# A block of their own for the turning products, ten tiles of P, and P V capped at three groups a block

## The chip, the cores and the metric

The kernel runs on one core of a Trainium2 chip. What counts is the device time of one execution in microseconds (us), as a median over runs. A core has five engines with queues of their own: TensorE (PE, with its weight loads shown apart as PEld), VectorE (DVE), ScalarE (ACT), GpSimd (POOL) and SyncE (SP), which here only issues transfers. Matrix products are written to PSUM, which has eight banks of 128 partitions by 512 float32; all other operands lie in SBUF.

## The reference

A transformer block with modulation by a condition vector: 2048 rows of 512 values, attention with 32 heads of 16, then a token mixer and an MLP. The parts around the change are those of the attention:

```python
h = _layernorm(x, axis=-1) * (1 + ca) + sa
qkv = (h @ wqkv).reshape(B, S, 3, H, Dh).transpose(2, 0, 3, 1, 4)
q, k, v = qkv[0], qkv[1], qkv[2]
p = _softmax(jnp.einsum("bhqd,bhkd->bhqk", q, k) * (Dh ** -0.5), axis=-1)
o = jnp.einsum("bhqk,bhkd->bhqd", p, v)
x = x + ga * (o.transpose(0, 2, 1, 3).reshape(B, S, D) @ wo)
```

After it, `x` goes through the second modulated layernorm and the mixer with its MLP (four more weight matrices), which the kernel calls the tail.

## The kernel before, in words

**Stages.** A prologue makes Q, K and V with their low parts and stores them to DRAM (`Qs`, `Ks`, `Vs`). Then comes the attention loop, which fills most of the time, and the tail in four chunks of 512 rows, of which the first one starts 30 steps before the attention ends.

**Units, steps, blocks.** The attention has 64 units: 4 chunks of 512 queries by 16 pairs of heads. A unit has 16 steps, one for each 128 keys (`NKT`), so there are 1024 steps, and a step has two halves, one for each head of the pair. The loop goes in blocks of three half steps (`GRP`). In a block PE does two things, one after the other:

- *rows* (`row_pair`): for each half step the scores S of this step (L1026, tile `sc`) and, 24 steps ahead, a product whose row maxima a later unit needs (L999, tile `mb`). Both use half of PE's rows and run side by side. Each writes a bank of its own out of seven that are shared (`sm`, `Slots`, tags s0 to s6).
- *columns* (`pv_part`): groups of P V, which lag behind by two blocks. A group is four products of 32 columns each, side by side. There is a group of the high part for every step (L1100) and one of the low part for every two steps (L1097). All of a unit add up in the eighth bank (tile `pv`, tag v).

The other engines empty the banks. DVE takes the maximum of each `mb` (L995). ACT takes the exponential of each `sc` into a tile of P (L1022). POOL makes the low part of P in place (L1075), or ACT does it (`p_low`) where the plan has POOL later. Tiles of P are a ring of six, and in the steps of `WIDE` (264 to 983) two more lie in tail buffers that are not yet in use (`xbs`), eight in all. The list `pvs` says in which order groups of P V come and from which half step on each may run; in `WIDE` a low part is put off by `LOWLAG` = 3 half steps more.

**The end of a unit.** After the last group of P V, ACT copies the sums from bank v to the tile `ac` (`ac_copy`, L1117), and the next unit's P V may write the bank. Four float32 products with the constant `smat` turn the sums into rows of queries (`o_fin`, L1127, tile `ot`). They stand in a generator that the plan lets go where PE has room and one of the seven shared banks is free, so they land behind the P V of some block, 1 to 12 us after `ac`. ACT then copies the result to `sm` (L1134), DVE takes the reciprocal `rc` (L1142), and POOL writes the output of the unit (L1138).

**Order.** All engines' instructions are put in order at build time by a planner (`Sched`) that carries a modelled time for each engine (`sch.T`), with planned costs. `crit` puts an instruction in its engine's queue at once; chains (`sch.chain`) and generators (`sch.add`) fill what is left. On the chip each engine keeps its order and waits on semaphores.

**Loads.** `before(s)` (L1600) puts in the loads on SP's queue: Q and K two units ahead at the first step of a unit (`load_unit`), V (`load_v`) six steps ahead of its unit. When a unit's maxima are known (`max_fin`), eight small transfers write the shift rows (`qtl<-nm`). K of a unit is first used 24 steps before the unit's scores. At step 884 a generator `tail_loads` (L1288) starts to load the tail's first things: three 1 MB pieces of weights (`wr`) on SP's queue, each `T0W` = 3000 ns of planned time after the other, and then four tiles `x1` of 256 KB on ACT's queue.

Of the kernel before, what the change touches and what calls it, by code (L numbers as in the profile page):

```python
# [8 lines left out]
F32 = mybir.dt.float32  # L9
# [3 lines left out]
I32 = mybir.dt.int32  # L13
# [28 lines left out]
PX = 270.0  # L42
XX = 170.0
XP = {"A": 280.0, "D": 200.0, "G": 200.0}
# [4 lines left out]
CROW, CCOL, CIN, CMID, COUT = 232.0, 240.0, 105.0, 95.0, 67.0  # L49
# [32 lines left out]
X1F = 6  # L82
# [1 line left out]
XBF = 4  # L84
XBT = 4
T0S = 30
T0L = 140
T0W = 3000.0
RATE3 = 1000.0
BURST3 = 1300.0  # L90
BF, BR = 2, 3
# [7 lines left out]
NPT = 6  # L99
# [7 lines left out]
LNC = 2  # L107
VP = 2
WIDE = range(S // CH * 64 + 8, 984)
LOWLAG = 3  # L110
XB = 4


# [219 lines left out]
def kernel(ctx, tc, A_x, A_wqkv, A_wo, B_w1, B_w2, B_w3, B_w4, c, w_mod, out):  # L333
    nc = tc.nc
    te, act, dve, pool, dma = nc.tensor, nc.scalar, nc.vector, nc.gpsimd, nc.sync
    x_d, out_d = A_x[0], out[0]
# [20 lines left out]
    def mark(key):  # L357
        return None, 0, lambda: done.add(key)
# [612 lines left out]
    def load_v(u):  # L971
        vst[u] = at.tile([P, NKT, 192], BF16, name="vst", tag="vst", bufs=2)
        sch.dma(dma.dma_start, vst[u], Vs[units[u][1]])

    sm = Slots(NSM)
    ptx = []
    e_exp, e_hi, e_low, v_free, acs = {}, {}, {}, [0.0], []

    def bank(nm):
# [23 lines left out]
    def new_pt(s):  # L1003
        if s in WIDE:
            i = pn[0] % (NPT + len(ptx)) - NPT
            pn[0] += 1
            if i >= 0:
                pt[s] = ptx[i]
                return
        pt[s] = at.tile([P, 2, CH], I32, name="pt", tag="pt", bufs=NPT)  # L1010

    def score_part(s, j):
# [97 lines left out]
    def ac_copy():  # L1110
        u, e = acs.pop()
        while u and ("ot", u - 1) not in done:
            sch.step()
        ac = at.tile([P, CH], F32, name="ac", tag="ac", bufs=1)
        vst.pop(u)
        acc = pv.pop(u)
        e = sch.crit("A", cA(), e + PX, lambda: act.activation(ac, acc, AF.Copy))  # L1117
        v_free[0] = e + XP["A"]
        sch.add(o_fin(u, ac, e + XP["A"]), 0)

    def o_fin(u, ac, ready):
        ci, pr = units[u]
        yield lambda: sch.T["P"] >= ready and sch.room()
        n = 2 * (DH + 1)
        b = dbank("ot")[:, :TPC * n]
        for t in range(TPC):
            te.matmul(b[:, t * n:(t + 1) * n], ac[:, t * P:(t + 1) * P], smat.rearrange("p j d -> p (j d)"), start=True, stop=True)  # L1127
            yield 110
        done.add(("ot", u))
        sm = at.tile([P, 8, DH + 1], F32, name="sm", tag="sm", bufs=2)  # L1130
        rc = at.tile([P, 8, 1], F32, name="rc", tag="rc", bufs=2)

        def sums():
            act.activation(sm.rearrange("p th d -> p (th d)"), b, AF.Copy)  # L1134
# [7 lines left out]
        sch.chain(("A", 170, sums), ("D", 90, lambda: dve.reciprocal(rc, sm[:, :, DH:DH + 1])), ("G", 350, fin),  # L1142
                  *([mark(("att", ci))] if pr == NP - 1 else []), prio=0, bank=b)


    GW = 130 + CH + 2
# [138 lines left out]
            for _ in mm3(b, wh[:, k, c], wl[:, k, c], A[:, k, 0, :n], A[:, k, 1, :n], k == 0, k == KT - 1):  # L1285
                yield nsq(n)

    def tail_loads():  # L1288
        rings["0"] = Ring(FRONT, [], "r")
        for _ in range(BR):  # L1290
            rings["0"].add([("wr", BR)])
            yield sch.wait(T0W)
        for t in range(TPC):
            x1t[t] = fa.tile([P, D], F32, name="x1", tag="x1", bufs=X1F)
            act.dma_start(x1t[t], x_d[t * P:(t + 1) * P])

    def tail(ci):
        end = ci == NC - 1
# [301 lines left out]
    def before(s):  # L1600

        nu, r = divmod(s + 32, 16)
        if r == 0 and 0 < nu < NU:
            ci, pr = units[nu]
            drain(("kq", pr // 4))
            if ci:
                drain(("q", pr // 8))
            load_unit(nu)
        nu, r = divmod(s + 6, 16)
        if r == 0 and 0 <= nu < NU:  # L1610
            drain(("v", units[nu][1] // 8))
            load_v(nu)
        if s == -12:
            unit_tiles(at, 2, dve, pool)

# [2 lines left out]
    blocks = [list(range(i, min(i + GRP, 2 * NS))) for i in range(-2 * LEAD, 2 * NS, GRP)]  # L1618
    pvs = []
    for s in range(0, NS, 2):  # L1620
        low = 2 * s + 2 + (min(LOWLAG, 2 * (NKT - 2 - s % NKT)) if s in WIDE else 0)
        pvs += [(2 * s, s, 0), (2 * s + 2, s + 1, 0), (low, s, 1)]
    pvs.sort(key=lambda x: x[0])
    due = 0.0
    for k, blk in enumerate(blocks + [[]] * (LAG + CPER)):
        if blk and blk[0] <= LENDS <= blk[-1]:
            sch.most = MOST
        for x in blk:
            if x % 2 == 0:
                if x == blk[0]:  # L1630
                    before(x // 2)
                if x >= 0 and x % 32 == 0:
                    drain(("shift", x // 32))
        if acs:
            ac_copy()
        row = [divmod(x, 2) for x in blk if x < 2 * NS]
        s0 = row[0][0] if row else 0
        col = []
        if k >= LAG and (k % CPER == 0 or not blk):

            x = (blocks[min(k - LAG, len(blocks) - 1)] or [-1])[-1]
            while pvs and pvs[0][0] < x and not (col and pvs[0][1] % NKT == 0 and not pvs[0][2]):
                col.append(pvs.pop(0)[1:])
        t, start = CIN, 0.0
        need = sum((s >= 0) + (s + LEAD < NS) for s, _ in row)
        sch.flush(need)
        banks = sorted(sm.t)
        n = 0
        for s, i in row:
            n += (s >= 0) + (s + LEAD < NS)  # L1650

            start = max(start, banks[n - 1 + 2 * (s < 0)] - t)
            t += CROW
        t += CMID
        for s, i in col:
            start = max(start, pv_ready(s, i) - t)
            t += CCOL
# [12 lines left out]
        sch.T["P"] += CMID  # L1670
        for s, i in col:
            pv_part(s, i)
        sch.T["P"] += COUT
        for e in "ADG":
            sch.misc(e, max(sch.T["P"], sch.T[e]) + TOLE[e])
        if s0 < 0:
            sch.fill(LEADB / 2 * len(blk))
        elif sch.gens:
            late = s0 >= NS - T0S
            due += RATE3 if late else RATE if s0 < NS // NC else RATE2  # L1680
            if due >= (BURST3 if late else BURST if s0 < NS // NC else BURST2):
                sch.fill(due)
                due = 0.0
        if 2 * (NS // NC) - 1 in blk:
# [12 lines left out]
            xnum = {"xn": 0, "xf": 0}  # L1697
            ptx += [xbs[:, 2 * i:2 * i + 2].bitcast(I32) for i in range(2)]
            big["A"] = big["A4"]
        if blk and blk[0] <= 2 * (NS - T0L) <= blk[-1]:  # L1700
            sch.add(tail_loads())
        if blk and blk[0] <= 2 * (NS - T0S) <= blk[-1]:
            sch.add(tail(0))
    if acs:
# [53 lines left out]
```

## Time and profile before

| What | us |
|---|---|
| median of 3 runs (2003.48 to 2003.94) | 2003.88 |
| the profiled execution | 2006.74 |
| its span, from the first instruction to the last | 2004.8 |
| DVE's maxima (L995), 2048 of 678 ns each, together | 1249.7 |
| ACT's exponentials (L1022), into the ring and into `xbs` | 890.3 + 200.0 |
| POOL's low parts (L1075), into the ring and into `xbs` | 1017.7 + 219.6 |
| busy in all: PE, DVE, ACT, POOL | 1939.3, 1656.6, 1519.9, 1551.9 |

Differences are made within the profiled execution; it took 2.9 us more than the median, 0.14%. Durations of instructions in a row overlap on an engine, so the distance from start to start tells what one costs in a run of them. In rows of the timeline, "x12" means that twelve instructions of one kind are drawn together, from the start of the first to the end of the last; the bracket at the end is the idle time before them with what ended it.

### The profile page before, as it was taken

How to read it: one execution, taken by the hardware profiler on the slowest of the kernel's cores; microseconds unless marked ns; L12 is line 12 of the kernel's file. 1: busy time of each engine (PE TensorE's matmuls, PEld its weight loads, DVE VectorE, ACT ScalarE, POOL GpSimd, SP SyncE). 2: the span in 40 equal slices, each digit the busy share in tenths (PEclk: the TensorE clock that was granted, in tenths of full speed). 3: DMA queues.
4: the chain of work that ended last, by engine and by line, in shares of the span. 5: the costliest groups of instructions: out<-in, count | busy, mean ns of one | idle time of the engine just before them, and what ended most of it. 6: DMA issues, size and time to landing. Idle time of an engine off the chain costs nothing.

```text
span 2004.8 us, 41627 instructions
## 1 busy us (share of the span) xinstructions
PE 1939.3 (97%) x14456; PEld 1161.6 (58%) x14456; DVE 1656.6 (83%) x2979; ACT 1519.9 (76%) x3100; POOL 1551.9 (77%) x1473
## 2 busy tenths in 40 slices
PE   7999999999999999999999999999998899999999
PEld 5755554554444444444444444444456788888998
DVE  6398888879999999999999999998976786656443
ACT  6438987768999999999999999998985545344443
POOL 6339998888999999999999999998995564435222
PEclk9989999999999999999999999999999999999999
DMA  8777665454444444444434343545415666553541
GB/s 292 235 196 190 158 177 175 131 135 124 94 83 97 87 94 90 91 91 90 94 87 95 86 96 85 107 115 128 94 38 213 225 235 266 217 205 112 199 152 69
DMA packets 185507, 277.99 MB, mean 139 GB/s; under 512 B 117105, under 2 KB 127857, under 8 KB 169009
## 3 DMA queue, kind: packets, MB, share of 16 engines
q1 hardware_dynamic: 181792, 267.20, 49.3%
q10 hardware_dynamic: 2304, 4.20, 0.6%
q0 software_dynamic: 1200, 3.93, 0.5%
q8 instruction: 115, 1.88, 0.4%
q14 instruction: 96, 0.78, 0.1%
HBM read 211.81 MB, written 62.91 MB: 137 GB/s over the span
## 4 chain that ended last, share of the span: by engine, by line
PE 61%; DVE 11%; DMA 4%; ACT 4%; POOL 3%; issue 2%; SPq 1%; ACTq 0%; POOLq 0%; DVEq 0%
PE mb L999 15%; PE sc L1026 10%; PE pv L1100 10%; DVE mx L995 8%; PE w L365 5%; PE w L361 5%; PE w L363 5%; PE pv L1097 4%; PE ot L1127 3%; ACT pt L1022 2%; DMA wr<-Ws 2%; POOL pt L1075 1%; PE xT L1261 1%; POOL trs L1370 1%; PE q L365 1%
## 5 line engine op out<-in xcount | busy, mean ns | idle before, releaser
L995 DVE TENSOR_REDUCE mx<-mb 128x1 f32<-128x512 f32 x2048 | 1249.7, 678 | 61.7 <-PE mb L999 54.0
L1075 POOL TENSOR_SCALAR pt<-pt 128x1024 f16<-128x1024 uint16 x773 | 1017.7, 1367 | 73.0 <-ACT pt L1022 72.6
L1022 ACT ACTIVATE pt<-sc 128x512 int32<-128x512 f32 x1688 | 890.3, 623 | 94.7 <-PE mb L999 65.6
L999 PE MATMUL mb<-kst,qtl 62*128 62x512 f32 x2048 | 787.0, 464 | 20.1 <-ACT pt L1022 7.7
L1026 PE MATMUL sc<-qtl,kst 64*128 64x512 f32 x2048 | 745.1, 451 | 3.7 <-DVE mx L995 1.8
L999 PEld LDWEIGHTS mb<-kst,qtl 62*128 62x128 f32 x2048 | 361.9, 193 | 263.3 <-ACT pt L1022 136.6
L1026 PEld LDWEIGHTS sc<-qtl,kst 64*128 64x128 f32 x2048 | 338.2, 185 | 189.2 <-DVE mx L995 116.9
L1100 PE MATMUL pv<-pt,vst 128*32 128x512 f16 x3376 | 318.6, 396 | 4.6 <-ACT ac L1117 4.6
L1479 POOL TENSOR_TENSOR g<-sq,g 128x256 fp32r<-128x256 f32 (+1 forms) x124 | 96.7, 784 | 189.7 <-ACT g L1478 176.0
L1075 POOL TENSOR_SCALAR xbs<-xbs 128x1024 f16<-128x1024 uint16 x165 | 219.6, 1363 | 4.4 <-ACT xbs L1022 4.3
L1022 ACT ACTIVATE xbs<-sc 128x512 int32<-128x512 f32 x360 | 200.0, 639 | 10.9 <-PE mb L999 9.5
L1100 PEld LDWEIGHTS <-vst 128*32 128x32 bf16 x4096 | 91.4, 94 | 182.9 <-issue 164.5
L1097 PE MATMUL pv<-pt,vst 128*32 128x512 f16 (+1 forms) x1688 | 173.0, 392 | 1.3 <-POOL pt L1075 1.3
L363 PE MATMUL w<-A,wr 128*128 128x256 f32 (+1 forms) x520 | 154.2, 297 | 0.3 <-DVE A L351 0.3
L361 PE MATMUL w<-A,wr 128*128 128x256 f32 (+1 forms) x520 | 154.2, 297 | 0.0
L365 PE MATMUL w<-A,wr 128*128 128x256 f32 (+1 forms) x520 | 154.0, 296 | 0.0
L1475 ACT ACTIVATE sq<-w 128x256 f32<-128x256 f32 (+1 forms) x130 | 52.0, 401 | 127.8 <-PE w L365 117.4
L361 PE MATMUL w<-wr,g 128*128 128x512 f32 x270 | 108.6, 402 | 3.0 <-DMA wr<-Ws 3.0
L365 PE MATMUL w<-wr,g 128*128 128x512 f32 x270 | 108.0, 400 | 3.1 <-POOL g L1479 3.1
L363 PE MATMUL w<-wr,g 128*128 128x512 f32 x270 | 107.7, 399 | 0.0
L1457 DVE SCALAR_TENSOR_TENSOR sq<-sq,w 128x256 f32<-128x256 f32 (+1 forms) x130 | 58.1, 449 | 55.6 <-ACT sq L1477 55.5
L363 PEld LDWEIGHTS w<-A,wr 128*128 128x128 f32 x520 | 99.6, 191 | 1.7 <-DVE A L351 0.5
(172 smaller groups left out, 2461.0 us busy)
## 6 DMA issues: line engine op xcount, KB each, us to landing
wr<-Ws SPq DMA_DIRECT2D x66, 1024.0 KB, 5.6
vst<-Vs SPq DMA_DIRECT2D x64, 768.0 KB, 5.2
kst<-Ks SPq DMA_DIRECT2D x126, 384.0 KB, 6.2
Ws<-wr SPq DMA_DIRECT2D x14, 1024.0 KB, 5.1
qtl<-Qs SPq DMA_DIRECT2D x128, 96.0 KB, 4.3
Vs<-vt SPq DMA_DIRECT2D x32, 384.0 KB, 4.3
Ks<-qk SPq DMA_DIRECT2D x16, 512.0 KB, 4.1
Qs<-qk SPq DMA_DIRECT2D x16, 512.0 KB, 3.0
```

What stands on the lines that cost most here:

```text
L361: te.matmul(o, lh, rh, start=first, stop=False)
L363: te.matmul(o, lh, rl, start=False, stop=False)
L365: te.matmul(o, ll, rh, start=False, stop=last)
L995: end = sch.crit("D", 605, e + PX, lambda: dve.reduce_max(mxs[u][:, j, g, c:c + 1], b, axis=AX.X))
L999: return ready, lambda: te.matmul(b, lhs, kst[u % 3][r, c * CH:(c + 1) * CH], start=True, stop=True), after
L1022: ea = sch.crit("A", 480, e + PX, lambda: act.activation(pt[s][:, j], b, AF.Exp))
L1026: return ready, lambda: te.matmul(b, kst[u % 3][r, kt * P:(kt + 1) * P], qst[u][r], start=True, stop=True), after
L1075: e_low[s] = XP["G"] + sch.crit("G", 1345, ready, lambda: pool.tensor_scalar(o, i, 0.5, 1.0, op0=OP.mult, op1=OP.mult))
L1097: te.matmul(acc[r:r + n, :], v[:, kt + i, c:c + n].bitcast(F16), pt[s + i].bitcast(F16)[:, j, 0::2], start=False, stop=kt == NKT - 2, skip ...
L1100: te.matmul(acc[r:r + 32, :], v[:, kt, r:r + 32], pt[s].bitcast(F16)[:, j, 1::2], start=kt == 0, stop=False, skip_group_check=True)
L1127: te.matmul(b[:, t * n:(t + 1) * n], ac[:, t * P:(t + 1) * P], smat.rearrange("p j d -> p (j d)"), start=True, stop=True)
L1479: ("G", cG(n), lambda: pool.tensor_tensor(lo, sq, hi, op=OP.subtract)), (None, 0, end), bank=b)
```

## The change

- A unit's turning products, for units 18 to 60 (`SUMS`), no longer go to the generator. They get an entry of their own in `pvs` behind the unit's last low part. A block whose columns begin with this entry has no other columns: rows, then the four products (`o_now`). They write the bank of the P V sums (tag v), so that the next unit's P V waits for ACT's copy `sm` instead of for `ac`, and comes one block later.
- A block takes at most three groups of P V (`COLS`) in the steps of `WIDE` but its last twelve; before, there was no cap.
- Two more tiles of P lie in the tail's buffers `xn` and `xf`: ten in all. The low part is put off by five half steps instead of three.
- The tail's first loads are tied to units: one `wr` piece behind V's load in each of the units 55, 56 and 57, and two `x1` tiles in each of 58 and 59.
- Planned entries that only mark something done, or that issue the shift rows, are looked at after every block in `WIDE` (`sch.marks()`).

```diff
-T0L = 140
-T0W = 3000.0
+T0U = (55, 56, 57, 58, 59)
...
+SUMS = range(18, 61)
+LOWLAG = 5
+COLS = 3
+CSUM = 900.0
...
-        sch.add(o_fin(u, ac, e + XP["A"]), 0)
+        if u in SUMS:
+            ots.append((u, ac))
+        else:
+            sch.add(o_fin(u, ac, e + XP["A"]), 0)
+
+    def o_sums(b, u, ac, t):
+        n = 2 * (DH + 1)
+        te.matmul(b[:, t * n:(t + 1) * n], ac[:, t * P:(t + 1) * P], smat.rearrange("p j d -> p (j d)"), start=True, stop=True)
+
+    def o_now():
+
+        u, ac = ots.pop()
+        b = ap_.tile([P, CH], F32, name="ot", tag="v", bufs=1)[:, :TPC * 2 * (DH + 1)]
+        e = sch.put("P", CSUM, 0.0, lambda: [o_sums(b, u, ac, t) for t in range(TPC)])
+        done.add(("ot", u))
+        sums, rest = o_rest(u, b)
+        v_free[0] = sch.crit("A", 170, e + PX, sums) + XP["A"]
+        sch.chain(*rest, prio=0, ready=v_free[0])
...
-    def tail_loads():
-        rings["0"] = Ring(FRONT, [], "r")
-        for _ in range(BR):
+    def tail_load(i):
+        if i == 0:
+            rings["0"] = Ring(FRONT, [], "r")
+        if i < BR:
             rings["0"].add([("wr", BR)])
-            yield sch.wait(T0W)
-        for t in range(TPC):
-            x1t[t] = fa.tile([P, D], F32, name="x1", tag="x1", bufs=X1F)
-            act.dma_start(x1t[t], x_d[t * P:(t + 1) * P])
+        else:
+            for t in range(2 * (i - BR), 2 * (i - BR) + 2):
+                x1t[t] = fa.tile([P, D], F32, name="x1", tag="x1", bufs=X1F)
+                act.dma_start(x1t[t], x_d[t * P:(t + 1) * P])
...
             load_v(nu)
+            if nu in T0U:
+                tail_load(nu - T0U[0])
...
-        low = 2 * s + 2 + (min(LOWLAG, 2 * (NKT - 2 - s % NKT)) if s in WIDE else 0)
+        low = 2 * s + 2 + (min(LOWLAG, 2 * (NKT - 2 - s % NKT)) if s in WIDE[:-12] else 0)
         pvs += [(2 * s, s, 0), (2 * s + 2, s + 1, 0), (low, s, 1)]
+        if s % NKT == NKT - 2 and s // NKT in SUMS:
+            pvs.append((low, s, 2))
...
-            while pvs and pvs[0][0] < x and not (col and pvs[0][1] % NKT == 0 and not pvs[0][2]):
+            while pvs and pvs[0][0] < x and not (col and (pvs[0][1] % NKT == 0 and not pvs[0][2] or pvs[0][2] > 1)) and not (
+                    pvs[0][1] in WIDE[:-12] and len(col) >= COLS):
                 col.append(pvs.pop(0)[1:])
+                if col[0][1] > 1:
+                    break
...
+        if s0 in WIDE:
+            sch.marks()
...
-            ptx += [xbs[:, 2 * i:2 * i + 2].bitcast(I32) for i in range(2)]
+            ptx += [x.bitcast(I32) for x in (xbs[:, 0:2], xbs[:, 2:4], xns["xn"][:, 0:2], xns["xf"][:, 0:2])]
```

More of the change, by code (lines that the diff above doesn't have):

```diff
@@ L109 @@
 WIDE = range(S // CH * 64 + 8, 984)
-LOWLAG = 3
+SUMS = range(18, 61)
+LOWLAG = 5
+COLS = 3
+CSUM = 900.0
 XB = 4
@@ L975 @@
     sm = Slots(NSM)
-    ptx = []
+    ptx, ots = [], []
     e_exp, e_hi, e_low, v_free, acs = {}, {}, {}, [0.0], []
@@ L1007, in new_pt @@
             if i >= 0:
+                assert all(v is not ptx[i] for v in pt.values())
                 pt[s] = ptx[i]
                 return
+        assert sum(all(v is not x for x in ptx) for v in pt.values()) < NPT
         pt[s] = at.tile([P, 2, CH], I32, name="pt", tag="pt", bufs=NPT)
@@ L1118, in ac_copy, with o_rest @@
         v_free[0] = e + XP["A"]
-        sch.add(o_fin(u, ac, e + XP["A"]), 0)
+        if u in SUMS:
[13 more added lines that the diff above has]
+        sch.chain(*rest, prio=0, ready=v_free[0])
     def o_fin(u, ac, ready):
-        ci, pr = units[u]
         yield lambda: sch.T["P"] >= ready and sch.room()
-        n = 2 * (DH + 1)
-        b = dbank("ot")[:, :TPC * n]
+        b = dbank("ot")[:, :TPC * 2 * (DH + 1)]
         for t in range(TPC):
-            te.matmul(b[:, t * n:(t + 1) * n], ac[:, t * P:(t + 1) * P], smat.rearrange("p j d -> p (j d)"), start=True, stop=True)
+            o_sums(b, u, ac, t)
             yield 110
         done.add(("ot", u))
+        sums, rest = o_rest(u, b)
+        sch.chain(("A", 170, sums), *rest, prio=0, bank=b)
+    def o_rest(u, b):
+        ci, pr = units[u]
         sm = at.tile([P, 8, DH + 1], F32, name="sm", tag="sm", bufs=2)
@@ L1140, in fin @@
                               rc.rearrange("p (t h) o -> p t h o", h=2).to_broadcast([P, TPC, 2, DH]), op=OP.mult)
-        sch.chain(("A", 170, sums), ("D", 90, lambda: dve.reciprocal(rc, sm[:, :, DH:DH + 1])), ("G", 350, fin),
-                  *([mark(("att", ci))] if pr == NP - 1 else []), prio=0, bank=b)
+        return sums, (("D", 90, lambda: dve.reciprocal(rc, sm[:, :, DH:DH + 1])), ("G", 350, fin),
+                      *([mark(("att", ci))] if pr == NP - 1 else []))
     GW = 130 + CH + 2
@@ L1655 @@
         for s, i in col:
-            start = max(start, pv_ready(s, i) - t)
-            t += CCOL
+            start = max(start, (pv_ready(s, i) if i < 2 else v_free[0]) - t)
+            t += CCOL if i < 2 else CSUM
         sch.gap(start)
@@ L1671 @@
         for s, i in col:
-            pv_part(s, i)
+            if i < 2:
+                pv_part(s, i)
+            else:
+                o_now()
         sch.T["P"] += COUT
@@ L1697 @@
             xnum = {"xn": 0, "xf": 0}
-            ptx += [xbs[:, 2 * i:2 * i + 2].bitcast(I32) for i in range(2)]
+            ptx += [x.bitcast(I32) for x in (xbs[:, 0:2], xbs[:, 2:4], xns["xn"][:, 0:2], xns["xf"][:, 0:2])]
             big["A"] = big["A4"]
-        if blk and blk[0] <= 2 * (NS - T0L) <= blk[-1]:
-            sch.add(tail_loads())
         if blk and blk[0] <= 2 * (NS - T0S) <= blk[-1]:
```

## The prediction

> **What bounds the kernel now.** I read the page first: PE is 97% busy and DVE, ACT and POOL 74 to 83%, over stages with different limits. So I took one steady stretch: units 19 to 55 of the attention, from one copy of the finished P V sums (`ac`) to the one 37 units later. The busy times by stretch (the columns are PE, PEld, DVE, ACT, POOL) and the instructions of the tile `ac` in it:
>
> ```profile
> 603.40:1339.70 736.30, 730.33 (x6222) 340.24 (x6218) 722.77 (x1259) 704.93 (x1396) 708.81 (x606) 1.00 0.44 92
> ```
> ```profile
> L1117 ACT ACTIVATE ac<-pv x38: 597/643/712, 603.4 to 1339.6; 128x512 f32<-128x512 f32 x38
> ```
>
> A unit takes (1339.6 - 603.4)/37 = 19.90 us. DVE is busy 98% of it, POOL 96%, ACT 96%. PE's 99% has overlapping and modelled ends, so I weigh PE by starts instead. How close DVE is to its limit, from the order of DVE's instructions:
>
> ```profile
> 808.84 0.17 DVE L1056 TENSOR_REDUCE mf<-mx 128x8 f32<-128x32 f32 x1
> 808.93 7.25 DVE L995 TENSOR_REDUCE mx<-mb 128x1 f32<-128x512 f32 x12
> ...
> 818.27 0.19 DVE L1142 RECIPROCAL rc<-sm 128x8 f32<-128x8 f32 x1
> 818.38 1.24 DVE L995 TENSOR_REDUCE mx<-mb 128x1 f32<-128x512 f32 x2
> ```
>
> Twelve maxima in a row take 7.25 us, two 1.24: one more costs (7.25 - 1.24)/10 = 0.60 us. A unit has 32 of them, one `mf` (0.09 to the next start) and one `rc` (0.11): 32 x 0.60 + 0.20 = 19.40 us. **DVE is the bound**; 19.90 - 19.40 = 0.50 us per unit is the time in which it is not fed. No change that leaves DVE's work alone can win more here.
>
> When is it not fed? A unit is 32 half steps and a block 3, so the pattern repeats every 3 units. In one such cycle the turning products (`ot`) fall into three blocks. PE, with the first starts of the blocks' rows of scores and maxima, of P V and of `ot`:
>
> ```profile
> 910.54 0.49 PE L1026 MATMUL sc<-qtl,kst 64*128 64x512 f32 x1
> ...
> 912.12 1.08 PE L1127 MATMUL ot<-smat,ac 128*128 128x34 f32 x8
> 913.12 0.50 PE L999 MATMUL mb<-kst,qtl 62*128 62x512 f32 x1
> ```
> ```profile
> 932.75 0.49 PE L1026 MATMUL sc<-qtl,kst 64*128 64x512 f32 x1
> ...
> 933.33 0.39 PE L999 MATMUL mb<-kst,qtl 62*128 62x512 f32 x1
> 933.65 0.41 PE L1100 MATMUL pv<-pt,vst 128*32 128x512 f16 x4
> ...
> 935.22 0.50 PE L999 MATMUL mb<-kst,qtl 62*128 62x512 f32 x1
> ```
> ```profile
> 938.70 0.50 PE L999 MATMUL mb<-kst,qtl 62*128 62x512 f32 x1
> ...
> 940.75 0.49 PE L1026 MATMUL sc<-qtl,kst 64*128 64x512 f32 x1
> ...
> 941.64 0.41 PE L1100 MATMUL pv<-pt,vst 128*32 128x512 f16 x4
> ...
> 942.99 0.50 PE L999 MATMUL mb<-kst,qtl 62*128 62x512 f32 x1
> ```
>
> and DVE over the same three places:
>
> ```profile
> 910.38 3.07 DVE L995 TENSOR_REDUCE mx<-mb 128x1 f32<-128x512 f32 x5
> 913.67 1.89 DVE L995 TENSOR_REDUCE mx<-mb 128x1 f32<-128x512 f32 x3 [0.22 <-PE mb L999]
> ```
> ```profile
> 932.38 3.06 DVE L995 TENSOR_REDUCE mx<-mb 128x1 f32<-128x512 f32 x5
> 935.76 1.89 DVE L995 TENSOR_REDUCE mx<-mb 128x1 f32<-128x512 f32 x3 [0.32 <-PE sc L1026]
> ```
> ```profile
> 938.23 4.96 DVE L995 TENSOR_REDUCE mx<-mb 128x1 f32<-128x512 f32 x8
> 943.53 1.89 DVE L995 TENSOR_REDUCE mx<-mb 128x1 f32<-128x512 f32 x3 [0.33 <-PE mb L999]
> ```
>
> Five maxima from 910.38 would let the next start at 910.38 + 5 x 0.60 = 913.38; it starts at 913.67: 0.29 us lost. In the same way 935.76 - 935.38 = 0.38 and 943.53 - 943.03 = 0.50. That is 1.17 us in three units, 0.39 per unit, **over three quarters of all that DVE loses**. A block needs 3 x 0.60 = 1.80 us of DVE. The blocks with `ot` take PE 2.58 and 2.47 us, and in the third case a block with four groups of P V (2.05) and one with `ot` (2.24) follow each other: too long by 0.78, 0.67 and 0.69. The banks filled ahead absorbed 0.49, 0.29 and 0.19 of it, 0.32 on average.
>
> There is one more loss, near the end of the attention. PE, then the copies `ac` of two units earlier and of this one, and the issues on SP:
>
> ```profile
> 1368.61 0.89 PE L999 MATMUL mb<-kst,qtl 62*128 62x512 f32 x2 [3.49 <-DMA kst<-Ks]
> ```
> ```profile
> 1339.61 0.64 ACT L1117 ACTIVATE ac<-pv 128x512 f32<-128x512 f32 x1
> ```
> ```profile
> 1385.16 0.70 ACT L1117 ACTIVATE ac<-pv 128x512 f32<-128x512 f32 x1
> ```
> ```profile
> 1353.16 0.59 SPq L137 DMA_DIRECT2D wr<-Ws  x1
> ...
> 1358.73 0.30 SPq L137 DMA_DIRECT2D kst<-Ks  x1
> ```
>
> PE waits 3.49 us for K: 1 MB of weights for the tail (`wr`) went out right ahead of K. The two units take 45.55 us where two take 39.80: **5.7 us lost**.
>
> **The change part by part.**
>
> *The products get a block of their own (43 units, 18 to 60).* Removed: four turning products behind the P V of some block, in one of the seven shared banks. Added: one block per unit with rows, no P V and the same four products, in the P V bank. No instruction is added on any engine; `ac`, `sm`, `rc` and the last product with `rc` stay. Moved are `ot` and `sm` to just behind `ac`, and P V by one block. What such a block takes: from first to last row start 933.33 - 932.75 = 0.58; from there to the first product is not in the trace. The row nearest to it is the way from rows to P V, 933.65 - 933.33 = 0.32, which I take; the bounds are 0.26 (a third of the 0.79 that three groups of P V take, below, as if nothing were switched) and 0.49 (902.40 to 902.89 below, where P V waited for `ac`). From the first product to the next rows: 913.12 - 912.12 = 1.00. Sum 1.90 us. The products also wait for `ac`, which now stands right before them. How long that is show two blocks in which P V waits for it now, the third row above (941.64 - 940.75 = 0.89) and this one:
>
> ```profile
> 900.90 0.41 PE L1097 MATMUL pv<-pt,vst 128*32 128x512 f16 x4
> ...
> 901.69 0.50 PE L999 MATMUL mb<-kst,qtl 62*128 62x512 f32 x1
> ...
> 902.40 0.50 PE L1026 MATMUL sc<-qtl,kst 64*128 64x512 f32 x1
> 902.89 0.63 PE L1100 MATMUL pv<-pt,vst 128*32 128x512 f16 x8
> ```
>
> 902.89 - 901.69 = 1.20. So the block takes 1.89 to 2.20 us, 0.09 to 0.40 more than DVE's 1.80. With 0.32 absorbed as now, 0 to 0.08 are left; I take 0.10 per unit instead of 0.39. That is 0.29 x 43 = 12.5 us.
>
> *At most three groups of P V a block.* Counted from the loop for units 18 to 60: now 329 blocks of two groups, 100 of three, 15 of four, 15 of one; then 189 of two, 213 of three, 15 of one, and the product blocks. A block of three takes 0.58 + 0.32 + (901.69 - 900.90 = 0.79) = 1.69 us, still 0.11 under DVE's 1.80. The four-group loss goes (it is in the 0.50 above). But behind the products stand two or more such blocks, which win back 0.11 each where two-group blocks win back some 0.3, and POOL, 96% busy, has to be faster too. For these I take a quarter off: **9.4 us**. Bounds: 0.50 x 43 = 21.5 (DVE never waits), and below nothing, as in the slower rival.
>
> *Ten P tiles, low parts two half steps later.* Alive at once are, by the same count, at most 9 instead of 8: no new wait. The wider lag covers the later P V; I cost it at nothing, hidden behind DVE.
>
> *The tail's loads.* Same bytes, placed at V's load in units 55 to 59: three `wr` on SP, then `x1` twice two on ACT's queue (its issues stand in ACT's order; ACT has 736 - 705 us of idle time in the stretch). SP's order then is K, V, `wr`, shift rows. Where V's load stands, and how long loads take:
>
> ```profile
> 916.13 0.42 SPq L137 DMA_DIRECT2D kst<-Ks  x1
> ...
> 921.82 0.34 SPq L137 DMA_DIRECT2D vst<-Vs  x1
> 929.89 0.47 SPq L137 DMA_DIRECT2D qtl<-nm  x1
> ```
> ```profile
> wr<-Ws SPq DMA_DIRECT2D x66, 1024.0 KB, 5.6
> vst<-Vs SPq DMA_DIRECT2D x64, 768.0 KB, 5.2
> ```
>
> V would land at 927.0 and `wr` behind it at 932.6 (estimate, one after the other), and the next K goes out at 916.13 + 19.9 = 936.0: free. The shift rows behind it leave only at 929.89. So the 5.7 us go, and nothing is late next.
>
> Sum: 9.4 + 5.7 = 15.1 us. The profiled execution took 2006.74 us (span 2004.8), 0.14% over the median of 2003.88; the differences are taken off the median: **1989 us**.
>
> **The rivals.**
>
> *The loads alone.* `ac` and the products in line on PE cost as much as the products at the end of P V do now (0.39 per unit stays, if ACT reaches `ac` some 0.3 later than in the rows above). For it: ACT is 96% busy. Against: the three `ac` blocks seen. 2003.9 - 5.7 = **1998**.
>
> *The new loads collide.* `wr` is still under way when K goes out, three times 1.9 us: the 5.7 come back, 2003.9 - 9.4 = **1994**. Against: the 3.4 us between 932.6 and 936.0; V goes out a block later, which eats 1.8 of them. [...]
>
> *P V waits for `sm`; slower.* The next unit's P V may write the bank only when ACT has copied `sm`, and PE keeps its order: rows behind a waiting P V wait too, then DVE. The rows of ACT around a turn now:
>
> ```profile
> 912.58 1.38 ACT L158 ACTIVATE pt<-pt 128x1024 f16<-128x1024 uint16 x1
> 913.80 0.28 ACT L1134 ACTIVATE sm<-ot 128x136 f32<-128x136 f32 x1
> ```
>
> `sm` starts 1.68 us after the first product, behind a low part on ACT, though the products had ended at 913.20. P V follows the first product by 1.00 + 0.58 + 0.32 = 1.90, so `sm` has to start by 1.62. With `ac` right ahead, three exponentials (3 x 0.5) put it at 1.5: just in time. With a low part too (1.2) it starts at 2.7, and P V waits 1.1. Then a unit loses 0.25 + 1.1 - 0.10 - 0.32 = 0.93 where it loses 0.39 now: 43 x 0.54 - 5.7 = +17, **2021**. From 0.7 us of waiting in every unit on the change is slower. Against: the planner books `ac` on ACT first and gives low parts to ACT only where POOL is later by 0.2 us or more. [...]
>
> **How the numbers follow.** Forecast (1979 to 1995, from 19 us of gain at the products to 3) 0.57; loads alone 0.20; loads collide 0.05; nothing that can be told 0.07; P V waits 0.11. A measurement of this kernel tells about 0.2%, 4 us, from no change. The first three are faster: 0.82; same 0.07; slower 0.11. The range runs from DVE's floor, nearly (2003.9 - 5.7 - 21.5 = 1977), past the loads alone to 2001; that leaves out the slower rival and part of no change.
>
> **What would show it.** Right: units of 19.6 to 19.7 us; DVE's gap beside `ot` at 0.1 or less; no wait for K near 1365; `ot` starting 0.3 to 0.5 after the last row. Wrong: P V waiting for `sm`; rows waiting for `ot`; POOL at 98% with P V waiting for low parts; K's wait anew after 1340.

## The result and the profile after

The changed kernel takes 2021.77 us (median of 5 runs, 2015.12 to 2023.19); the kernel before took 2003.88 in the same series (5 runs, 2000.79 to 2005.48). The ratio is 1.0087, 95% interval 1.0068 to 1.0106: **slower by 0.9%**, where 1989 was forecast. From the page of the changed kernel:

```profile
span 2019.7 us, 41648 instructions
...
PE 1942.4 (96%) x14456; PEld 1161.0 (57%) x14456; DVE 1659.9 (82%) x2979; ACT 1524.0 (75%) x3100; POOL 1555.9 (77%) x1473
```

The shares have hardly moved. Where the time went is seen in the stretch in which the change works, units 19 to 55, as in the prediction. From the table by stretch (PE, PEld, DVE, ACT, POOL) and from the groups of instructions:

```profile
606.40:1360.30 753.90, 736.94 (x6214) 344.34 (x6216) 726.62 (x1258) 708.72 (x1396) 709.33 (x605) 0.99 0.43 92
```
```profile
L1121 ACT ACTIVATE ac<-pv x38: 595/617/692, 606.4 to 1360.3; 128x512 f32<-128x512 f32 x38
```

A unit takes (1360.3 - 606.4)/37 = 20.38 us, 0.48 more than before; 19.6 to 19.7 was expected. DVE is idle for 753.9 - 726.6 = 27.3 us of the stretch where it was for 736.3 - 722.8 = 13.5. The bound was named rightly, but DVE is now fed worse, not better. What it waits for, in the waits of that stretch (us in total, times, longest):

```profile
DVE rc L1166 <- ACT sm L1158: 10.0, 13, 1.2
DVE mx L997 <- PE mb L1001: 9.1, 37, 0.9
DVE mx L997 <- PE sc L1030: 2.6, 4, 1.1
```

The first line is new. It belongs to the block of products. PE and DVE over such a block, in order of time:

```profile
1137.35 0.51 PE L1001 MATMUL mb<-kst,qtl 62*128 62x512 f32 x1
...
1138.81 1.08 PE L1130 MATMUL ot<-smat,ac 128*128 128x34 f32 x8
1139.82 0.49 PE L1030 MATMUL sc<-qtl,kst 64*128 64x512 f32 x1
```
```profile
1136.66 3.11 DVE L997 TENSOR_REDUCE mx<-mb 128x1 f32<-128x512 f32 x5
1140.50 0.20 DVE L1166 RECIPROCAL rc<-sm 128x8 f32<-128x8 f32 x1 [0.72 <-ACT sm L1158]
```
```profile
1138.07 0.68 ACT L1121 ACTIVATE ac<-pv 128x512 f32<-128x512 f32 x1
...
1139.98 0.41 ACT L1158 ACTIVATE sm<-ot 128x136 f32<-128x136 f32 x1
```

From rows to rows the block takes 1139.82 - 1137.35 = 2.47 us, since the products wait for `ac`. DVE had five maxima from 1136.66 and could have gone on at 1139.66; `rc` starts at 1140.50, so 0.84 us are lost. The next two blocks of products in DVE's order:

```profile
1155.79 3.68 DVE L997 TENSOR_REDUCE mx<-mb 128x1 f32<-128x512 f32 x6 [0.19 <-PE mb L1001]
1159.57 0.20 DVE L1166 RECIPROCAL rc<-sm 128x8 f32<-128x8 f32 x1
...
1175.02 5.07 DVE L997 TENSOR_REDUCE mx<-mb 128x1 f32<-128x512 f32 x8
1180.10 0.20 DVE L1166 RECIPROCAL rc<-sm 128x8 f32<-128x8 f32 x1
```

They lose 1159.57 - 1159.39 = 0.18 and 1180.10 - 1179.82 = 0.28. Three units lose 1.30 us at the block, 0.43 a unit: **as much as the products lost at their old place (0.39)**. The other 0.5 us a unit are lost elsewhere, which the experiments take apart.

The tail's loads did what was expected. PE's longest wait from 1340 to 1440, where K had cost 3.49 us, is now:

```profile
PE sc L1030 <- DMA qtl<-nm: 0.9, 1, 0.9
```

### The profile page after: what moved, and what is told of

The parts are those of the page before. It is cut to its first block, busy times and chain, and to the rows that moved or that the text cites. A ratio compares the mean times of both kernels' runs of the same rounds, so it can differ in the third digit from the quotient of the medians.

```text
span 2019.7 us, 41648 instructions
## 1 busy us (share of the span) xinstructions
PE 1942.4 (96%) x14456; PEld 1161.0 (57%) x14456; DVE 1659.9 (82%) x2979; ACT 1524.0 (75%) x3100; POOL 1555.9 (77%) x1473
## 4 chain that ended last, share of the span: by engine, by line
PE 60%; DVE 18%; ACT 10%; issue 5%; POOL 3%; DMA 3%; SPq 1%; ACTq 0%; POOLq 0%; DVEq 0%
DVE mx L997 14%; PE mb L1001 12%; PE sc L1030 10%; PE pv L1104 9%; ACT pt L1026 6%; PE w L367 5%; PE w L365 5%; PE w L363 5%; PE pv L1101 4%; PE ot L1130 2%; PE xT L1285 1%; POOL pt L1079 1%; SPq L139 1%; DMA wr<-Ws 1%; ACT xbs L1026 1%
## 5 line engine op out<-in xcount | busy, mean ns | idle before, releaser
L1079 POOL TENSOR_SCALAR pt<-pt 128x1024 f16<-128x1024 uint16 x682 | 901.3, 1370 | 72.6 <-ACT pt L1026 71.6
L1026 ACT ACTIVATE pt<-sc 128x512 int32<-128x512 f32 x1472 | 771.7, 615 | 100.6 <-PE mb L1001 65.0
L1104 PE MATMUL pv<-pt,vst 128*32 128x512 f16 x2944 | 277.7, 398 | 5.8 <-ACT ac L1121 5.8
L1079 POOL TENSOR_SCALAR xbs<-xbs 128x1024 f16<-128x1024 uint16 x127 | 169.6, 1363 | 7.3 <-ACT xbs L1026 7.2
L1026 ACT ACTIVATE xbs<-sc 128x512 int32<-128x512 f32 x288 | 155.8, 615 | 10.8 <-PE mb L1001 6.1
L1101 PE MATMUL pv<-pt,vst 128*32 128x512 f16 x1472 | 151.7, 392 | 1.4 <-POOL pt L1079 1.3
```

Of the source, the lines that this page charges most:

```text
L1026: ea = sch.crit("A", 480, e + PX, lambda: act.activation(pt[s][:, j], b, AF.Exp))
L1079: e_low[s] = XP["G"] + sch.crit("G", 1345, ready, lambda: pool.tensor_scalar(o, i, 0.5, 1.0, op0=OP.mult, op1=OP.mult))
L1101: te.matmul(acc[r:r + n, :], v[:, kt + i, c:c + n].bitcast(F16), pt[s + i].bitcast(F16)[:, j, 0::2], start=False, stop=kt == NKT - 2, skip ...
L1104: te.matmul(acc[r:r + 32, :], v[:, kt, r:r + 32], pt[s].bitcast(F16)[:, j, 1::2], start=kt == 0, stop=False, skip_group_check=True)
```

## The experiments

Each was run with the kernel before on the same chip (medians of 2001.5 to 2003.0), and the ratio is to that one. Diffs with "+" and "-" are against the kernel that the text names.

### Three suspicions from the trace of after

First, the shift rows (`nm` into `qtl`), whose last transfer lands some 1.9 us after the start of the first scores in one unit of three (2.1 us at most); then DVE's wait in front of `rc`; then the block itself; and the loads alone.

`e1_shift_early`, against the changed kernel: the chain that makes the shift rows goes ahead of other waiting work, and its transfers go out right behind V's load.

```diff
-                    if start + ch[1][0][1] <= until + AGE * ...
+                    if start + ch[1][0][1] <= until + URGENT * (ch[2] < 0) + AGE * ...
...
-                  (None, 0, shift_rows), mark(("shift", u)), prio=0, ready=sch.T["D"])
+                  (None, 0, shift_rows), mark(("shift", u)), prio=-1, ready=sch.T["D"])
```

> The changed kernel with one thing different: the small chain that makes the shift rows (mf, two copies on ACT, one step on POOL, eight transfers) may be put into ACT's queue up to 1.5 us of planned time earlier; its transfers stay behind V's load on SP. Theory S (shift rows late): in two of three units the second scores of a new unit wait 0.8 to 1.9 us for the last shift row, because ACT's copies now come 2.2 to 2.7 us behind mf where they came 0.2 to 1.2 behind it before. Then the waits go, and with them the half-rate stretches of the clock that follow them: 2021.8 less 13 to 18 us, 2004 to 2009. Theory R (the reciprocal blocks DVE) and theory P (the block with the products is too long for PE) expect no gain: 2019 to 2023.

Measured: 2023.24 us, ratio 1.0110 [1.0092, 1.0128]. The shift rows land before the first scores now in all but one unit of the change, and nothing is gained. The clock is no higher: in pieces of 200 us from 600 to 1400 it is 0.99, 0.99, 0.98 and 0.99, where the changed kernel has 0.99, 0.99, 0.99 and 1.00.

`e2_rc_later`, against the changed kernel: `rc` may be placed only 1.5 us after `sm` in the plan.

```diff
-        sch.chain(*rest, prio=0, ready=v_free[0])
+        sch.chain(*rest, prio=0, ready=v_free[0] + RCW)
```

> The changed kernel with DVE's reciprocal rc placed 1.5 us of planned time later, so that DVE doesn't stand at it waiting for sm. Theory R: DVE is kept from maxima that lie ready, 11.5 us in units 18 to 60; the time falls by some 10 us, to 2011. Theory P: the maxima behind rc are not ready either, because PE's rows come late behind the products; at most 3 us fall away, 2018 to 2022, and the same idle time is then put down to mb and sc. Theory S expects no change.

Measured: 2018.23 us, 1.0078 [1.0061, 1.0095]. A wait of 10 us gives back 3.5 at most, and the intervals of the two kernels overlap. The line with `rc` is gone from DVE's waits, but the wait for `mb` has grown from 9.1 us to 19.5: the maxima behind `rc` weren't ready either.

```profile
DVE mx L998 <- PE mb L1002: 19.5, 58, 1.1
```

`e3_no_block`, against the changed kernel: `SUMS = range(0)`, so the products stay at their old place; lag, tiles, cap and loads as changed.

> The changed kernel with no unit in SUMS: the products go to the generator as before; ten tiles, the cap of three groups, the wider lag and the moved loads stay. If the block of products is what costs (theories P and S, which comes with it), this is at or under the kernel before: 1996 to 2004. If the tiles, the cap or the lag cost, it stays above 2010.

Measured: 2024.32 us, 1.0115 [1.0097, 1.0133]. Taking the block out of the changed kernel gains nothing.

`e4_loads_only`: the kernel before with `tail_load` in units 55 to 59 and nothing else of the change.

> The kernel before with only the tail's loads tied to units 55 to 59. All theories: the wait for K near 1365 us goes and nothing comes in its place, 5.7 us less: 1998. If the new place collides with K it stays at 2003 or more.

Measured: 1995.54 us, 0.9970 [0.9957, 0.9982]. The loads gain 6.5 us where 5.7 were worked out. It **beats both kernels**, and what follows is counted from it. A unit takes (1337.5 - 600.9)/37 = 19.91 us in it, and DVE is idle for 736.8 - 722.7 = 14.1:

```profile
600.80:1337.60 736.80, 730.82 (x6222) 340.74 (x6219) 722.66 (x1259) 705.00 (x1396) 708.54 (x606) 1.00 0.44 94
```
```profile
L1116 ACT ACTIVATE ac<-pv x38: 597/642/712, 600.9 to 1337.5; 128x512 f32<-128x512 f32 x38
```

So the rest of the change costs 26 us by the medians and 23 by the ratios, and no single suspicion holds them.

### One part at a time

`f2_cap`, on the loads alone: no block takes more than three groups of P V.

```diff
-            while pvs and pvs[0][0] < x and not (col and pvs[0][1] % NKT == 0 and not pvs[0][2]):
+            while pvs and pvs[0][0] < x and not (col and pvs[0][1] % NKT == 0 and not pvs[0][2]) and not (
+                    pvs[0][1] in WIDE[:-12] and len(col) >= COLS):
```

> The kernel before with the loads tied to units 55 to 59 (e4_loads_only, 1995.5 us) and one thing more: no block takes more than three groups of P V (COLS 3). Eight tiles of P, a lag of 3, the turning products where they were. Theory C (the cap is what costs: a group that a block may not take waits for the next block, so P V falls behind and meets the unit's end): 2008 to 2020. Theory L (the longer lag with ten tiles is what costs) and theory B (the block of turning products costs, and what the kernel without it lost was something else): 1993 to 1998.

`f3_lag5`, on the loads alone: `LOWLAG = 5`, ten tiles, `WIDE[:-12]`.

> The kernel before with the loads tied to units 55 to 59 (1995.5 us) and the longer lag: LOWLAG 5 instead of 3, ten tiles of P instead of eight, the last twelve steps of the wide stretch without a lag; no cap, no block. Theory L: 2008 to 2020, with the first P V of a unit waiting for the copy of the sums (0.9 us a time, as in 18 of some 40 units of the kernel without the block). Theories C and B: 1993 to 1998.

`g1_after_lag3`, against the changed kernel: `LOWLAG = 3`.

> The changed kernel with LOWLAG back at 3 and nothing else changed (block, cap and ten tiles stay); only the order on TensorE differs. Theory L: 1993 to 2002. Theory C: 2018 to 2024, as the changed kernel. Theory B: 2018 to 2024.

`g3_block_alone`, against the changed kernel: `LOWLAG = 3`, no cap, eight tiles, no `sch.marks()` behind the blocks.

> The changed kernel with the cap, the longer lag, the two more tiles and the marks taken back: the block of turning products and the moved loads alone. Theories C and L: the block does what the prediction said by itself or nothing, 1985 to 1997. Theory B: 2010 to 2022.

Measured: the cap 2107.60 (1.0525 [1.0505, 1.0545]), the lag 2189.82 (1.0940 [1.0919, 1.0961]), the changed kernel with the old lag 2029.75 (1.0127 [1.0104, 1.0150]), the block 2073.86 (1.0352 [1.0329, 1.0375]). Three parts are far slower alone than the whole change, which no theory had. One line of PE's waits in `g3_block_alone` (from 600 to 1360) says why, and SP's order there in one unit:

```profile
PE sc L1030 <- DMA qtl<-nm: 54.5, 6, 9.4
```
```profile
896.82 0.30 SPq L139 DMA_DIRECT2D qtl<-Qs  x1
...
898.11 0.41 SPq L139 DMA_DIRECT2D kst<-Ks  x1
898.61 8.25 SPq L139 DMA_DIRECT2D qtl<-nm  x8
```

Six times PE waits some 9 us for the shift rows, which a unit needs at once, because they stand behind the Q and K loads of a later unit, and those wait until their buffer is free (from 606 to 1400 SP's longest wait for PE's `mb` and for its `sc` is 13.7 us; for `mb` it is 1.7 in the changed kernel). The marks are what puts them in front: without the change the planner gets to them only where it looks for other work to fill in, with it after every block. The prediction never mentioned that line of the diff. It is no gain by itself (`h4_tiles_marks` below has it on the loads alone, with two more tiles, and its trace has every engine's instructions in the order of `e4_loads_only`), but the other parts need it. So each part was run again with it.

`g4_block_marks`: `g3_block_alone` with the marks.

> The block of turning products and the moved loads with the marks put back (after every block of the wide stretch the planner issues what is due, so the eight shift-row transfers go out ahead of the next unit's Q and K loads): eight tiles, lag 3, no cap. In the run without the marks the first scores waited 54.5 us in 6 waits for the shift rows. Theory M (that wait and the half-rate clock behind it were all that the block alone lost): its undisturbed units took 60.14 us for three, 0.16 a unit more than the 59.67 of the kernel with only the loads moved, so 2000 to 2005. Theory B (the block costs by itself as much as the whole change): 2015 to 2024. If the block gains as predicted: 1984 to 1990.

`f6_cap_marks` and `f7_lag5_marks`: `f2_cap` and `f3_lag5` with the marks.

> The moved loads, the cap of three groups a block and the marks; no block, eight tiles, lag 3. Theory C (the cap costs even with the transfers in time): its units between the long waits took about 20.4 us, 0.5 more than without a cap, over 42 units: 2012 to 2020. If the cap cost only by the late transfers: 1994 to 1999.

> The moved loads, the lag of 5 with ten tiles and the marks; no cap, no block. Theory L (the longer lag costs even with the transfers in time): its units between the long waits took about 20.45 us: 2012 to 2022. If the lag cost only by the late transfers: 1994 to 1999.

`g5_after_nocap`: the changed kernel without the cap.

> The changed kernel without the cap of three groups: block, lag of 5, ten tiles, marks and loads stay. Theory C: 1998 to 2006. Theory L: 2015 to 2024. If cap and lag mend in the change what the block spoils: above 2024.

`h4_tiles_marks`, on the loads alone: ten tiles and the marks, the lag left at 3.

> The kernel before with the moved loads, ten tiles of P instead of eight and the marks, the lag left at 3. It parts f7_lag5_marks (2029.6 us): if the two more tiles cost nothing, as predicted, 1993 to 1998, and all 34 us of that run belong to the lag; if the tiles cost (they lie elsewhere in SBUF), above 2005.

Measured, with the difference to the loads alone (1995.5):

| block | lag 5 | cap | us | ratio | difference |
|---|---|---|---|---|---|
| - | - (ten tiles) | - | 1996.91 | 0.9964 [0.9953, 0.9975] | +1 |
| yes | - | - | 2003.59 | 1.0009 [0.9998, 1.0021] | +8 |
| - | - | yes | 2010.95 | 1.0052 [1.0036, 1.0069] | +15 |
| - | yes | - | 2029.60 | 1.0142 [1.0125, 1.0159] | +34 |
| yes | yes | - | 2014.06 | 1.0056 [1.0037, 1.0076] | +19 |
| - | yes | yes | 2024.32 | 1.0115 [1.0097, 1.0133] | +29 |
| yes | - | yes | 2029.75 | 1.0127 [1.0104, 1.0150] | +34 |
| yes | yes | yes | 2021.77 | 1.0087 [1.0068, 1.0106] | +26 |

The differences are between medians of several series; by the ratios they come to -1, 8, 16, 34, 17, 29, 31 and 23 us. Only the tiles are free. Every other part costs by itself, and they don't add: the lag costs 34 us alone and 10 beside the block. On the way from the loads to the whole change, block, lag and cap cost 8, 10 and 8 (8, 9 and 6 by the ratios; the intervals of the last step overlap).

### Why the block gains nothing

`h1_one_product`, on the loads alone, with the order of every engine kept:

```diff
         for t in range(TPC):
-            te.matmul(b[:, t * n:(t + 1) * n], ...)
+            if t == 0 or u not in ONE:
+                te.matmul(b[:, t * n:(t + 1) * n], ...)
```

> The kernel before with the moved loads, and of a unit's four turning products only the first, in units 18 to 60 (the copy of the sums reads the first product four times over): the order on every engine is that of e4_loads_only, three quarters of the products' own time is gone. It measures what the prediction sold: 0.39 us of VectorE lost a unit beside the products. Theory T (that loss is the products' time on TensorE): three quarters of 0.39 over 43 units, 12.6 us, so 1981 to 1986 beside 1995.5. Theory O (the loss belongs to the order around the unit's end, the copy of the sums and the wait of the reciprocal, and the products only share it): 1991 to 1996.

Measured: 1993.65 us, 0.9954 [0.9940, 0.9969]. This run decides. DVE with all products (`e4_loads_only`) over the three places of a cycle:

```profile
966.33 4.26 DVE L994 TENSOR_REDUCE mx<-mb 128x1 f32<-128x512 f32 x7
970.82 1.89 DVE L994 TENSOR_REDUCE mx<-mb 128x1 f32<-128x512 f32 x3 [0.22 <-PE mb L998]
...
990.71 1.87 DVE L994 TENSOR_REDUCE mx<-mb 128x1 f32<-128x512 f32 x3
992.91 1.89 DVE L994 TENSOR_REDUCE mx<-mb 128x1 f32<-128x512 f32 x3 [0.33 <-PE sc L1025]
...
994.83 5.52 DVE L994 TENSOR_REDUCE mx<-mb 128x1 f32<-128x512 f32 x9
1000.69 1.89 DVE L994 TENSOR_REDUCE mx<-mb 128x1 f32<-128x512 f32 x3 [0.34 <-PE mb L998]
```

and with one of four (`h1_one_product`), at the same instructions:

```profile
964.13 6.06 DVE L995 TENSOR_REDUCE mx<-mb 128x1 f32<-128x512 f32 x10
970.11 0.19 DVE L1143 RECIPROCAL rc<-sm 128x8 f32<-128x8 f32 x1
970.23 6.25 DVE L995 TENSOR_REDUCE mx<-mb 128x1 f32<-128x512 f32 x10
...
992.14 3.62 DVE L995 TENSOR_REDUCE mx<-mb 128x1 f32<-128x512 f32 x6
996.21 3.68 DVE L995 TENSOR_REDUCE mx<-mb 128x1 f32<-128x512 f32 x6 [0.45 <-PE mb L999]
999.81 0.19 DVE L1143 RECIPROCAL rc<-sm 128x8 f32<-128x8 f32 x1
```

The gaps beside the products are gone, as they should be: ten maxima in one piece where 0.29 us were lost, six where 0.46 were. But two new ones stand there: 0.2 us within the ten from 970.23, and 996.21 - (992.14 + 3.60) = 0.47 in front of the last products, where nothing was lost before. It is so in the whole stretch: added up in the same way, each of its 12 cycles of three units loses 0.29, 0.42 and 0.42 us beside the products with all four, and with one of four nothing there, but 0.27 behind a block with three groups of P V and 0.49 behind the one with four. The second of these, on PE and its weight loads:

```profile
993.23 0.50 PE L999 MATMUL mb<-kst,qtl 62*128 62x512 f32 x1
...
994.63 0.41 PE L1100 MATMUL pv<-xbs,vst 128*32 128x512 f16 x4
...
995.65 0.49 PE L1026 MATMUL sc<-qtl,kst 64*128 64x512 f32 x1
```
```profile
993.70 0.19 PEld L999 LDWEIGHTS mb<-kst,qtl 62*128 62x128 f32 x1 [0.17 <-ACT pt L1022]
994.19 0.19 PEld L999 LDWEIGHTS mb<-kst,qtl 62*128 62x128 f32 x1 [0.30 <-ACT pt L1022]
```

This block takes 995.65 - 993.23 = 2.42 us, where the same one takes 2.03 with all products (995.85 to 997.88): two of its rows wait for ACT's exponentials, and then come four groups. The groups of `ac` say what is left:

```profile
L1117 ACT ACTIVATE ac<-pv x38: 598/635/712, 601.2 to 1333.4; 128x512 f32<-128x512 f32 x38
```

(1333.4 - 601.2)/37 = 19.79 us a unit, 0.12 under 19.91. Three quarters of 0.39 would have been 0.29. Over the 43 units the gain is 1.9 us by the medians, 3.2 by the ratios and 5.2 by the units (0.12 x 43); three quarters of the loss would have been 12.6.

`h2_block_one_product`: the same on `g4_block_marks`.

> The block of turning products with the marks (g4_block_marks, 2003.6 us), with only the first of the four products in units 18 to 60, in the same order. If the block's length is what costs (1.9 to 2.1 us where VectorE has 1.8 us to do; the three products are some 0.6 us of it): 1988 to 1994. If the P V groups that the block pushes into the next blocks (4 and 5 groups, 2.0 and 2.6 us) and the first scores cost: 1999 to 2003.

Measured: 2009.02 us, 1.0031 [1.0019, 1.0042], not below the 2003.59 with four products. The block has become short (1.38, 1.66 and 1.46 us on average for the three units of a cycle, where it took 2.06, 2.24 and 1.99), but ACT's `sm` starts no sooner after the first product, and DVE waits for it in front of `rc` 7.9 us in the stretch, as against 8.1. So the block's own length alone isn't what costs; a short block together with a late `rc` was not tried.

`h3_block_shift_early`: `g4_block_marks` with the edit of `e1_shift_early`.

> The block of turning products with the marks (2003.6 us) and the shift rows' chain moved ahead of other waiting work (as in e1_shift_early, where the transfers then landed before the first scores and nothing was gained). The first scores of two units in six wait here (slack -1.34 and -0.76 us; VectorE loses 0.36 and 0.25 us in their blocks). Theory S (the shift rows cost the block's gain): 1996 to 2000. Theory O (order: what is gained there is lost at the next place): 2001 to 2007.

Measured: 2021.41 us, 1.0092 [1.0076, 1.0108], 17 us slower by the ratios. That work moved forward for one wait is missing at another fits; at which one was not followed.

`i2_block_cap4`: `g4_block_marks` with a cap of four groups, so that the block's displaced P V never makes a block of five.

> g4_block_marks (2003.6 us: loads, block, marks) with at most four groups of P V a block, so that none has five (2.61 us on average, one in three units). If the groups that the product block pushes out cost: one third of 0.8 us over 43 units is 11 us at most, some of it given back as four-group blocks: 1995 to 2001. If the loss only moves: 2002 to 2012.

Measured: 2004.31 us, 1.0014 [1.0003, 1.0024]: no change. The loss moves. There is no block of five, but one wait in PE's list has grown from 5.0 us in 6 waits (`g4_block_marks`) to

```profile
PE pv L1104 <- ACT sm L1158: 10.1, 12, 0.9
```

In one unit of three `sm` starts 2.4 us after the first product, and the next unit's P V waits for it, the wait that the prediction's slower rival names.

`i1_lag5_not_at_end`: `f7_lag5_marks` with the lag at 3 for the last three low parts of a unit; only PE's order differs.

```diff
-        low = 2 * s + 2 + (min(LOWLAG, 2 * (NKT - 2 - s % NKT)) ...
+        low = 2 * s + 2 + (min(LOWLAG if s % NKT < NKT - 6 else 3, 2 * (NKT - 2 - s % NKT)) ...
```

> f7_lag5_marks (2029.6 us: loads, ten tiles, marks, lag 5) with the lag back at 3 for the last three low parts of each unit; only TensorE's order differs from it. Theory E (the lag costs by what it gathers at the unit's end, where a block with three groups and the products takes 2.98 us): 1996 to 2010. Theory A (it costs by the order that the planner then makes on the other engines, where the products and their reciprocal stand elsewhere): 2022 to 2032.

Measured: 2034.81 us, 1.0160 [1.0146, 1.0174]. The lag's cost isn't gathered at the unit's end. It fits that it lies in the order that the planner makes on the other engines: beside the lag of 3 with ten tiles (`h4_tiles_marks`), ACT, POOL and DVE have another order in the trace, while in the changed kernel, where the lag changes PE's order alone (`g1_after_lag3`), the lag of 5 is the faster one by 8 us. Which displaced instruction begins it stays open. DVE's waits with the lag of 5, beside those with ten tiles and the lag of 3 (in its 735.5 us from 602.2):

```profile
DVE mx L994 <- PE mb L998: 21.9, 62, 0.8
DVE rc L1141 <- ACT sm L1133: 6.5, 12, 0.6
DVE mx L994 <- PE sc L1025: 5.5, 13, 0.7
```
```profile
DVE mx L994 <- PE mb L998: 10.6, 35, 0.4
DVE mx L994 <- PE sc L1025: 1.4, 6, 0.3
```

It isn't one long wait but twice as many short ones, spread over the unit.

## Why the prediction was wrong

**The bound** (DVE, 19.40 us of 19.90) was right; units of every kernel here stay above it. (ACT and POOL are 76 and 77% busy on the page before; the "74" is a slip on which nothing rests.)

**The loads** were right: 5.7 us expected, 6.5 measured, no wait for K left.

**"I take 0.10 per unit instead of 0.39. That is 0.29 x 43 = 12.5 us" failed, twice over.** First, the step before it, "With 0.32 absorbed as now": the block's length was right (2.47, 1158.88 - 1156.93 = 1.95 and 1179.54 - 1177.64 = 1.90 us against 1.89 to 2.20, one of them over), too long by 0.67, 0.15 and 0.10. But DVE lost 0.84, 0.18 and 0.28: not 0.32 absorbed but 0.13 a block lost on top of the excess. `rc` stands in front of the maxima and waits for `sm`; with `rc` out of the way (`e2_rc_later`) DVE waited for the maxima instead (19.5 us for `mb`, up from 9.1), so the banks held no reserve when the block came. Second, the ground under it: that a loss which stands beside the products is the products' price. `h1_one_product` took three quarters of their time away, with no block and no changed order, and a unit gained 0.12 us of the 0.29. The prediction had the sign of this in its hands: POOL and ACT at 96% of the stretch. With four engines between 96 and 99%, the gaps that closed here (0.29 to 0.42 us) came back in other places (0.27 and 0.49): behind rows that waited for ACT and PE's blocks of three and four groups of P V.

**"I cost it at nothing, hidden behind DVE", the lag, failed**: 34 us alone, 10 beside the block. The count of the tiles was right (+1 us); what two half steps do to the order of ACT, POOL and DVE was never counted; that this is what costs fits, and is not shown.

**The quarter off for the cap** allowed for a cost and had the wrong size: 15 us alone, 8 on top of block and lag. The 1.69 us for a block of three, 0.11 under DVE's 1.80, hold only where nothing keeps its rows: the 183 such blocks in the stretch of the changed kernel take 1.87 us on average (median 1.74).

**The slower rival** gave 2021, and 2021.77 came, but not by its mechanism. P V doesn't wait for `sm` in the changed kernel; DVE's `rc` does, and moving it gives back 3.5 us at most. The rival's wait is there in the kernels with the block and without the cap of three, 8.8 us in 12 waits in `g5_after_nocap`, which is still faster than the changed kernel.

**What was not in it at all** is the line with the marks, which holds the order of SP's queue, and on which 70 us of the block alone hang (2073.9 - 2003.6): in the traces of these two runs PE, DVE and POOL have the same order, and on SP only the shift rows, Q and K change places.

## What to carry over

An idle gap beside an instruction needn't be that instruction's price. Where several engines are as busy as here (96 to 99% of the stretch), leave the instruction out in its old place and time that, before building it a new place: one run told that three of the four products gave 2 to 5 us, where 12.6 was their share of the loss. In an order written out by hand, every shift of a queue position is a part of the change that can have a price of its own, also the line that only flushes what is due: 70 us of the block alone hung on it.

## What the runs showed of the hardware

The long waits of PE in `g3_block_alone` cost more than their length. That kernel by stretches around one 9 us wait for the shift rows; the granted clock is the third column from the end:

```profile
888.00:898.00 10.00, 9.85 (x88) 3.92 (x84) 9.78 (x18) 9.27 (x20) 10.00 (x11) 1.00 0.01 4
898.00:907.00 9.00, 0.00 (x0) 0.00 (x0) 1.17 (x2) 0.20 (x1) 2.43 (x2) 0.74 0.69 110
907.00:919.00 12.00, 11.78 (x86) 5.74 (x86) 8.99 (x16) 9.66 (x19) 7.86 (x7) 0.77 0.21 67
919.00:929.00 10.00, 9.83 (x82) 4.09 (x80) 10.00 (x18) 9.57 (x21) 9.72 (x10) 1.00 0.06 1
```

The clock falls to 0.74 in the wait and is 0.77 in the 12 us after it, where PE has work again: DVE is busy 9.0 us of these 12, and 10.0 of the 10 behind them. Such waits make up 54.5 of the 70 us; what is left, 2.6 us a wait, is about the 3.0 us that DVE is idle in those 12.

The changed kernel loses clock without any such wait. Three stretches in a row, the first two at full clock; the block of products is at the end of the second (its `ot` from 892.65):

```profile
886.97:890.39 3.42, 3.42 (x33) 1.59 (x32) 3.42 (x6) 3.42 (x6) 2.57 (x3) 1.00 1.02 187
890.39:893.81 3.42, 3.29 (x22) 1.92 (x23) 3.22 (x6) 3.42 (x8) 3.42 (x4) 1.00 0.67 176
893.81:897.22 3.41, 3.41 (x22) 1.48 (x24) 1.96 (x4) 2.01 (x5) 3.41 (x4) 0.50 0.23 95
```

The clock is 0.50 for 3.41 us, and DVE is busy for 1.96 of them. It happens again at 770.93 and 1016.69, 122.88 us to either side, and not once in this part of the kernel before, where the clock is 1.00 from 600 to 1367. No wait of PE longer than 0.2 us is listed around the three (880 to 900, 765 to 776, 1008 to 1022), and the stretches ahead of them have PE busy for 3.29 of 3.42, 3.28 of 3.41 and 3.28 of 3.41 us. The one shown has fewer matmuls (22, where the one before has 33), among them eight small products. That these do it fits and isn't shown. Half clock comes without them, too. This is `h2_block_one_product`, with two small products instead of eight, and the stretch ahead:

```profile
745.59:749.00 3.41, 2.48 (x18) 1.38 (x20) 3.41 (x7) 3.41 (x8) 2.61 (x3) 1.00 0.70 233
749.00:752.41 3.41, 3.41 (x28) 1.32 (x22) 1.55 (x4) 2.01 (x6) 2.95 (x3) 0.50 0.00 0
```

`e3_no_block` has two behind stretches with no product at all (from 1314.98 and 1386.66; its clock from 1200 to 1400 is 0.98). In these stretches PE stands still for 0.8 to 1.2 us at a time. So half clock came here behind stretches with PE busy for 2.26 of 3.41 us (583.20 to 586.61 in the changed kernel, with a wait of 1.2 for `ac`), for 2.48 and for 3.28; what in them decides stays open.
